# Row scaling, expert outputs and the first two units put in another order in a one-core attention, mixture-of-experts and feed-forward kernel

## The chip, the cores and the metric

The kernel runs on one core of one Trainium2 chip, in one launch. The metric is the device time of that launch in microseconds (us). Its inputs and its output lie in the chip's memory; weights are read in fp32.

## What is computed

The reference has three stages, one behind the other, over 1536 tokens (2 sequences of 768) of 512 features (8 heads of 64):

```python
# 1. linear attention with a decaying state, token by token
state = gamma * state + outer(k[t], v[t]);   y[t] = scale * (q[t] @ state)
# 2. mixture of experts: one of 8 for each token, at most `capacity` tokens each
e = argmax(x @ w_gate);  gate = softmax(x @ w_gate)[e]
out = gate * (relu(x @ w1[e]) @ w2[e])            # 512 -> 1024 -> 512
# 3. feed-forward with a rational activation
h = x @ w_in                                      # 512 -> 2048
g = (a0 + a1*h + a2*h^2 + a3*h^3) / (1 + |b0|*|h| + |b1|*h^2 + 1e-6)
out = g @ w_out                                   # 2048 -> 512
```

## The kernel before, in words

Everything runs in one hand-ordered program: the order in which the Python code calls the engines is the order of each engine's queue, and each engine takes its queue strictly in turn. The engines are TensorE (PE, with its weight loads as PEld), VectorE (DVE), ScalarE (ACT), GpSimd (POOL), and SyncE (SP), whose queue issues most transfers.

**Attention** works on 12 units of 128 tokens (`attention`, L614). A unit has a features part (k and q, transposed; chunk 0 of `kv`, 512 KB) and a tokens part (v, then k; chunk 1, 512 KB). Unit 0 takes its v from the table `c0`, so it needs only the k half of chunk 1 (`attn_part(0, 3)`, 256 KB). SP asks for these in a written order: features of unit 0, `c0`, the k half of unit 0, features of unit 1, the v half and the k half of unit 1 as two transfers, features of unit 2, then tables and the rest. For unit u, PE does: `inter(u)` (queries times the state, into `yt`; not for unit 0), `intra(u)` (v times the masked scores, into `yt`), `state(u)` (k times v, added to `st`, which ACT then copies to `s`), `scores(u + 1)` (into `sc`). DVE masks the scores (`scm`, L321 and L329) and POOL scales the v half of each unit (L278); `intra` needs both.

**Experts** (`moe`, L972). Expert 0 is done apart (`first_expert`); its last 96 rows leave it as `y0`. Experts 1 to 7 take 224 slots each. The rows of an expert are gathered by POOL, scaled with the gate by ACT (`x_gate`, L954, two parts j of 128 and 96 rows), and transposed by PE into a PSUM bank (`expert_x`, `tp`, L964), from which ACT makes the rounded high part `xh` and DVE the rest `xl` (L967, L968). All products are made of three matmuls on such high and low parts. An expert has four steps fp of the first layer (L994 to L996, ACT and DVE make `h` in L999 and L1000) and four steps q of the second (into two PSUM tiles `acc`, L373, called from L1021). Beside each step a half of the weights of later experts is split (`prep_next`: ACT L149, DVE L154), and a slice of the feed-forward weights is decoded (`dec_slot`). In expert e, `x_gate(e + 1, 0)` stands at fp 0 and `x_gate(e + 1, 1)` at fp 2; `expert_x(e + 1, ...)` at fp 1 and fp 3. `y_turn(y0, 1)` stands at fp 0 of expert 1: it transposes `y0` on PE into `ytp` (L850), in the same single PSUM bank (kind `xt`) that `expert_x` uses from expert 2 on, and ACT and DVE read it (L856, L857). Behind q 3, `y_pair` moves each `acc` to the expert's place among the features `yh` and `yl`: one ACT copy (L856) and two DVE operations (L857, L859) per `acc`. A branch for overfull experts (`overflow`, L1047, not taken here) stands behind q 3 of expert 3.

**Feed-forward** (`ffn_step(n)`, n = 0 to 47). Step n has 12 matmuls of the first layer (`ffn_a`, L1116 to L1118, into `h`, four banks in turn), the activation in pieces (`ffn_i` on ACT: L1129 to L1131; `ffn_p` on DVE and POOL: L1140 to L1142; `ffn_r` on ACT: L1147, L1148; `ffn_e` on DVE: L1153 to L1155; `ffn_g` on ACT and POOL: L1165, L1167), each some steps behind, and 12 matmuls of the second layer for step n - 5 (`ffn_b`, L1187 to L1189, into `o`). A bank of `h` is free when `ffn_e` has read it. Steps 0 to 3 are woven into q 0 to q 3 of expert 7. Expert 7 differs from the others: its `y_pair(0)`, `ffn_step(4)` and `y_pair(1)` come behind the loop, in this order. Then the experts' PSUM tiles are given up and the banks for `o` are opened in their place, and `ffn` goes on with step 5, whose `ffn_b(0)` is the first to write an `o`.

Of the kernel before, what the change touches and what calls it, by code (L numbers as in the profile page):

```python
# [7 lines left out]
F32 = mybir.dt.float32  # L8
# [5 lines left out]
AF = mybir.ActivationFunctionType  # L14
ALU = mybir.AluOpType
# [6 lines left out]
E = 8  # L22
# [62 lines left out]
class Build:  # L85
# [528 lines left out]
    def attention(self):  # L614
        nc, tc, a = self.nc, self.tc, self.a
        with ExitStack() as st:
            self.ap = self.pool("attn", stack=st)
            self.pa = self.pool("pa", space=PSUM, stack=st)
            self.kv, self.sc, self.scm, self.s, self.yt, self.xt = {}, {}, {}, {}, {}, {}
            self.route, self.place, self.xk, self.rk, self.where = {}, {}, {}, {}, {}  # L620
            self.qd, self.yp = {}, {}
            n0, n1 = self.cols["ident"][0], self.cols["tri"][0]
            nk = self.cols["gk"][0]
            self.c0 = self.ap.tile([128, -(-(nk + H * D) // 32) * 32], F32, name="c0")[:, 0 : nk + H * D]
            self.ca = self.ap.tile([128, -(-(n0 - nk) // 32) * 32], F32, name="ca")[:, 0 : n0 - nk]
            self.wi = self.ap.tile([128, 4, 256], F32, name="wi")[:, :, 0:136]
            self.tri = self.ap.tile([128, 128], BF16, name="tri")
            self.ones = self.ap.tile([128, 128], BF16, name="ones")
            self.lgs = self.ap.tile([128, NU, 4, E], F32, name="lgs")
            self.xg0 = self.ap.tile([128, DM], F32, name="xg0")  # L630
            self.x0 = [self.ap.tile([128, 4, 128], F32R, name=n) for n in ("xh0", "xl0")]
            self.wu = self.ap.tile([128, 128], BF16, name="wu")
            self.attn_load(0, 0)
            nc.sync.dma_start(out=self.c0, in_=a["c0"])
            self.attn_part(0, 3)
            self.attn_load(1, 0)
            self.attn_part(1, 2)
            self.attn_part(1, 3)
            self.attn_load(2, 0)
            nc.sync.dma_start(out=self.ca[:, 0 : n1 - nk], in_=a["ct"][:, nk:n1])  # L640
            nc.sync.dma_start(out=self.ct, in_=a["ct"][:, n0:])
            self.attn_load(2, 1)
            for c in range(2):
                self.attn_load(3, c)
            nc.sync.dma_start(out=self.ca[:, n1 - nk :], in_=a["ct"][:, n1:n0])
            dve, pool = nc.vector, nc.gpsimd
            dve.memset(self.wu, 0.0)
            dve.memset(self.ones, 1.0)
            self.warm(WA)
            self.scores(0)  # L650
            self.mask_first()
            for h in (0, 4):
                self.scale(0, pool, slice(h, h + 4))
            self.y_table(0, pool)
            self.scale(1, pool)
            self.y_table(1, pool)
            self.warm(WC)
            ident = self.col("ident").unsqueeze(1).to_broadcast([128, 4, 128])
            wg = self.col("wg").rearrange("p (k e) -> p k e", e=E)
            done = {GROUPS[b + 1] - 1: b for b in range(len(GROUPS) - 1)}  # L660
            for u in range(NU):
                last = u == NU - 1
                if u + 4 < NU:
                    for c in range(2):
                        self.attn_load(u + 4, c)
                self.load_next(LOADS[u])
                if u + 2 < UA + 3:
                    self.scale(u + 2, pool)
                if u + 2 < UPB:
                    self.y_table(u + 2, pool)  # L670
                for n in LO_AT.get(u, ()):
                    self.split_lo(n // 2, n % 2)
                if 3 < u < NU - 1:
                    self.scores(u + 1)
                    self.mask(u + 1)
                if u - 2 in done:
                    next(gate)
                self.inter(u)
                if u - 4 in done:
                    self.place_first()  # L680
                if u == 3:
                    self.scores(u + 1)
                    self.mask(u + 1)
                self.intra(u)
                if u:
                    self.attn_xt(u)
                if u - 2 in done:
                    next(gate)
                self.state(u)
                if u < 3:  # L690
                    self.scores(u + 1)
                    self.mask(u + 1, 1 if u else 2)
                if u == 0:
                    self.attn_xt(0)
                    nc.scalar.activation(out=self.wi[:, :, 0:128], in_=ident, func=AF.Copy)
                    nc.scalar.activation(out=self.wi[:, :, 128:], in_=wg, func=AF.Copy)
                if u == 3:
                    nc.scalar.activation(out=self.tri, in_=self.col("tri"), func=AF.Copy)
                    nc.scalar.activation(out=self.b0a, in_=self.ab[:, 4:5], func=AF.Abs)
                    nc.scalar.activation(out=self.b1a, in_=self.ab[:, 5:6], func=AF.Abs)  # L700
                    nc.vector.memset(self.cq, 1.0 + 1e-6)
                if u:
                    self.gate_mm(u - 1)
                if u - 2 in done and not last:
                    self.rank_mm(done[u - 2])
                if 0 < u < NU - 1:
                    self.gate_out(u - 1, (0,))
                for n in LO_MID.get(u, ()):
                    self.split_lo(n // 2, n % 2)
                if u - 1 in done:  # L710
                    gate = self.gate_parts(done[u - 1])
                    next(gate)
                if 0 < u < NU - 1:
                    self.gate_out(u - 1, (1,))
                if UA + 3 <= u + 2 < NU:
                    self.scale_heads(u + 2)
                for n in HI_AT.get(u, ()):
                    self.split_hi(n // 2, n % 2)
                if u - 2 in done and not last:
                    self.rank_pos(done[u - 2])  # L720
                if u - 3 in done and not last:
                    self.rank_put(done[u - 3])
                    self.gate_put(done[u - 3])
                for n in LO_END.get(u, ()):
                    self.split_lo(n // 2, n % 2)
            self.attn_tail()
# [123 lines left out]
            self.nc.tensor.transpose(tp[:, k], y[:, k * 128 : k * 128 + 128], self.col("ident")[0:r, 0:r])  # L850
        self.y_put(tp, slice(0, 4), bass.ds(self.start(0), r) if j else slice(0, r))

    def y_put(self, ps, k, at, more=None):
        yh, yl = self.yh[:, k, at], self.yl[:, k, at]
        tt = self.nc.vector.tensor_tensor
        self.nc.scalar.activation(out=yh, in_=ps, func=AF.Copy)  # L856
        tt(out=yl if more is None else yl.bitcast(F32), in0=ps, in1=yh.bitcast(F32), op=ALU.subtract)  # L857
        if more is not None:
            tt(out=yl, in0=more, in1=yl.bitcast(F32), op=ALU.add)  # L859

    def start(self, e):
        lo, hi = (max(0, NT - (E - e) * W), NT) if e else (0, 128)
# [109 lines left out]
    def moe(self):  # L972
        nc = self.nc
        with ExitStack() as st:
# [8 lines left out]
            for e in range(1, E):  # L983
                xh, xl = (t.pop(e)[:, :, 0:W] for t in (self.xh, self.xl))
                h = {}
                for fp in range(4):
# [14 lines left out]
                        out=hl, in0=ps, scalar=0.0, in1=hh.bitcast(F32), op0=ALU.max, op1=ALU.subtract  # L1001
                    )
                    self.prep_next()
                    if fp < 3 and fp != 1 and e + 1 < E:
                        self.x_gate(e + 1, fp // 2)
                    if fp % 2 and e + 1 < E:
                        self.expert_x(e + 1, fp // 2)
                        if e + 2 < E:
                            self.gather(2 * (e + 2) + fp // 2)
                    self.dec_slot(8 * e + fp)  # L1010
                    if (e, fp) == (1, 0):
                        self.y_turn(self.y0, 1)
                acc = [self.wide(i, "acc").rearrange("p (o n) -> p o n", o=2)[:, :, 0 : 2 * W] for i in range(2)]
                acc = [t.rearrange("p o (a n) -> p o a n", a=2) for t in acc]
                for q in range(4):
# [13 lines left out]
                        self.perm_get()  # L1029
                    if q == 3:  # L1030
                        at = bass.ds(self.start(e), W)
                        for i in range(2 if e < E - 1 else 0):
                            self.y_pair(acc, i, at)
                    self.dec_slot(8 * e + 4 + q)
                    if e == E - 1:
                        self.ffn_step(q)
                    if q % 2:
                        del self.whi[4 * e + 2 + q // 2], self.wlo[4 * e + 2 + q // 2]
            for i in range(2):
                self.y_pair(acc, i, at)  # L1040
                if i == 0:
                    self.ffn_step(4)

    def y_pair(self, acc, i, at):
        self.y_put(acc[i][:, :, 0], slice(2 * i, 2 * i + 2), at, acc[i][:, :, 1])

    def overflow(self):  # L1047
        nc, tc = self.nc, self.tc
# [179 lines left out]
    def ffn(self):  # L1228
        with ExitStack() as st:
            self.fp = self.pool("ffn", stack=st)  # L1230
            self.pf = self.pool("pf", space=PSUM, stack=st)
            for n in range(5, NA):
                self.ffn_step(n)
            self.ffn_tail()

# [178 lines left out]
```

## Time and profile before

| | before |
|---|---|
| median of 3 runs (lowest, highest) | 514.39 us (513.76, 514.82) |
| the profiled execution's own time | 512.93 us |
| its span, first to last instruction | 511.2 us |
| PE busy | 496.5 us, 97% of the span |
| DVE, ACT, POOL busy | 413.9, 365.4, 243.5 us |
| mean granted clock of PE | 0.996 of full speed |

Busy time of an engine is the time in which one of its instructions runs. Idle time counts for the end of the program only on an engine that has no idle time to spare later, so the table is read together with the rows below, which say where PE stands still and what it waits for.

### The profile page before, as it was taken

The numbers are of one execution on the slowest core, as the hardware profiler recorded it, in microseconds if no ns is written. First come the engines' busy times: TensorE is split into PE (matmuls) and PEld (weight loads), VectorE is DVE, ScalarE is ACT, GpSimd is POOL, SyncE is SP. The second block draws the span as 40 slices with busy tenths as digits, with TensorE's granted clock in tenths as the row PEclk, the third lists the DMA queues.
The fourth block names the chain that finished last, engine by engine and source line by source line (L and its number), as shares of the span: only waits on it lengthen the run. The fifth ranks groups of instructions, "written<-read, shape, count | busy, mean of one in ns | idle before, by whom it ended". The sixth has DMA issues, their size and how long they took to land.

```text
span 511.2 us, 9195 instructions
## 1 busy us (share of the span) xinstructions
PE 496.5 (97%) x3401; PEld 430.9 (84%) x3401; DVE 413.9 (81%) x602; ACT 365.4 (71%) x605; POOL 243.5 (48%) x187
## 2 busy tenths in 40 slices
PE   8999999999999999999879999999999999999995
PEld 5888878999999999998668888888888888888883
DVE  2579858789997999894686989999899998865973
ACT  1356638868767677664857989989999987776760
POOL 2621041034243744543424547667568764354774
PEclk9999999999999999999989999999999999999999
DMA  8999676899987999971400002222013100000203
GB/s 304 408 414 388 215 226 205 325 324 297 320 298 225 382 306 269 322 243 30 164 0 2 0 4 79 83 82 83 27 58 113 52 1 0 2 1 0 83 21 144
DMA packets 27409, 83.07 MB, mean 163 GB/s; under 512 B 4960, under 2 KB 5216, under 8 KB 27360
## 3 DMA queue, kind: packets, MB, share of 16 engines
q1 hardware_dynamic: 24304, 73.52, 42.2%
q0 software_dynamic: 2624, 7.35, 4.1%
q10 hardware_dynamic: 432, 1.57, 1.0%
q8 instruction: 27, 0.44, 0.3%
q14 instruction: 22, 0.18, 0.1%
HBM read 71.94 MB, written 10.49 MB: 161 GB/s over the span
## 4 chain that ended last, share of the span: by engine, by line
PE 62%; DVE 3%; ACT 2%; POOL 1%; issue 1%; POOLq 0%; ACTq 0%; DVEq 0%
PE h L1116 8%; PE h L1117 8%; PE h L1118 8%; PE o L1187 8%; PE o L1188 8%; PE o L1189 8%; PE acc L373 7%; PE e L996 2%; PE e L995 2%; PE e L994 2%; POOL out L1218 1%; PE tp L964 1%; DVE fw L1153 1%; DVE h L1154 1%; ACT fx L1129 0%
## 5 line engine op out<-in xcount | busy, mean ns | idle before, releaser
L154 DVE TENSOR_TENSOR wlo<-raw,whi 128x1024 fp32r<-128x1024 f32 x80 | 112.5, 1418 | 12.8 <-ACT whi L149 12.3
L1167 POOL TENSOR_TENSOR gg<-fx,gg 128x512 fp32r<-128x512 f32 x47 | 61.0, 1299 | 76.1 <-issue 60.8
L149 ACT ACTIVATE whi<-raw 128x1024 fp32r<-128x1024 f32 x80 | 83.2, 1056 | 2.0 <-PE acc L373 1.3
L1187 PE MATMUL o<-whi,gg 128*128 128x512 f32 x192 | 75.5, 393 | 4.6 <-DVE yl L859 4.6
L1188 PE MATMUL o<-wlo,gg 128*128 128x512 f32 x192 | 75.2, 392 | 0.0
L1189 PE MATMUL o<-whi,gg 128*128 128x512 f32 x192 | 75.2, 392 | 0.0
L1116 PE MATMUL h<-yh,whi 128*128 128x512 f32 x192 | 74.8, 390 | 0.0
L1118 PE MATMUL h<-yh,wlo 128*128 128x512 f32 x192 | 74.8, 389 | 0.0
L1117 PE MATMUL h<-yl,whi 128*128 128x512 f32 x192 | 74.7, 389 | 0.0
L373 PE MATMUL acc<-h,whi 128*128 128x448 f32 x224 | 71.3, 377 | 0.0
L1142 POOL TENSOR_TENSOR fw<-fh,fw 128x512 f32<-128x512 f32 x48 | 64.2, 1338 | 12.8 <-ACT fw L1131 12.0
L1129 ACT ACTIVATE fx<-h,ct 128x512 f32<-128x512 f32 x48 | 37.3, 777 | 42.9 <-PE h L1118 41.2
L209 POOL TENSOR_TENSOR gq<-gq 128x512 int32<-128x512 int32 x16 | 26.9, 1684 | 85.0 <-DVE gq L206 38.7
L994 PE MATMUL e<-xh,whi 128*128 128x224 f32 x224 | 62.1, 277 | 0.1
L996 PE MATMUL e<-xh,wlo 128*128 128x224 f32 x224 | 61.5, 274 | 0.0
L995 PE MATMUL e<-xl,whi 128*128 128x224 f32 x224 | 61.5, 274 | 0.0
L373 PE MATMUL acc<-h,wlo 128*128 128x224 f32 x224 | 59.0, 263 | 0.0
L1187 PEld LDWEIGHTS o<-whi,gg 128*128 128x128 f32 x192 | 36.4, 190 | 13.0 <-ACT fh L1130 5.0
L373 PEld LDWEIGHTS acc<-h,whi 128*128 128x128 f32 x224 | 42.0, 187 | 3.2
L994 PEld LDWEIGHTS e<-xh,whi 128*128 128x128 f32 x224 | 43.0, 192 | 0.5 <-ACT yh L856 0.4
L1153 DVE SCALAR_TENSOR_TENSOR fw<-fw,cq,h 128x512 f32<-128x512 f32 x48 | 35.6, 741 | 9.7 <-ACT h L1148 9.7
L995 PEld LDWEIGHTS e<-xl,whi 128*128 128x128 f32 x224 | 43.0, 192 | 0.0
(167 smaller groups left out, 1111.3 us busy)
## 6 DMA issues: line engine op xcount, KB each, us to landing
raw<-wm SPq DMA_DIRECT2D x61, 512.0 KB
r<-wf SPq DMA_DIRECT2D x32, 512.0 KB
kv<-kv SPq DMA_DIRECT2D x22, 512.0 KB
wd<-gq SPq DMA_DIRECT2D x16, 256.0 KB
raw<-wd SPq DMA_DIRECT2D x8, 512.0 KB
xd<-xs SPq DMA_DIRECT2D x12, 256.0 KB
raw<-wm ACTq DMA_DIRECT2D x3, 512.0 KB
kv<-kv SPq DMA_DIRECT2D x3, 256.0 KB
```

Of the source, the lines that this page charges most:

```text
L149: nc.scalar.activation(out=self.whi[i][:, sl], in_=raw, func=AF.Copy)
L154: (eng or self.nc.vector).tensor_tensor(out=self.wlo[i][:, sl], in0=raw, in1=self.whi[i][:, sl].bitcast(F32), op=ALU.subtract)
L373: self.nc.tensor.matmul(out, lhsT=w, rhs=x, start=start, stop=stop, skip_group_check=True)
L994: nc.tensor.matmul(ps[:, fi], lhsT=wh[:, sl], rhs=xh[:, k], start=(k == 0), stop=False)
L995: nc.tensor.matmul(ps[:, fi], lhsT=wh[:, sl], rhs=xl[:, k], start=False, stop=False)
L996: nc.tensor.matmul(ps[:, fi], lhsT=wl[:, sl], rhs=xh[:, k], start=False, stop=(k == 3))
L1116: nc.tensor.matmul(h, lhsT=wh[:, sl], rhs=self.yh[:, k, ts], start=(k == 0), stop=False)
L1117: nc.tensor.matmul(h, lhsT=wh[:, sl], rhs=self.yl[:, k, ts], start=False, stop=False)
L1118: nc.tensor.matmul(h, lhsT=wl[:, sl], rhs=self.yh[:, k, ts], start=False, stop=(k == 3))
L1187: self.nc.tensor.matmul(ps, lhsT=gh[:, ms], rhs=wh[:, ws], start=first, stop=False)
L1188: self.nc.tensor.matmul(ps, lhsT=gh[:, ms], rhs=wl[:, ws], start=False, stop=False)
L1189: self.nc.tensor.matmul(ps, lhsT=gl[:, ms], rhs=wh[:, ws], start=False, stop=last)
```

## The change

Four edits, in the order of the program:

- Start: SP asks for unit 1's features ahead of the k half of unit 0, and for unit 1's tokens as one transfer of 512 KB in the place of two of 256 KB. On PE `scores(1)` (and its mask on DVE) stands ahead of `state(0)`.
- Row scaling: `x_gate(e, 0)` for e from 3 on stands at q 2 of expert e - 2, and no longer at fp 0 of expert e - 1. `x_gate(2, 0)` stays at fp 0 of expert 1, behind `dec_slot`.
- `y_turn(y0, 1)` moves from fp 0 to q 0 of expert 1.
- Experts' end: `y_pair` is divided into `y_high` (the ACT copy) and `y_low` (the two DVE operations). For experts 1 to 6 the order on each engine is as before. For expert 7 both copies stand ahead of `ffn_step(3)`, all four DVE operations right behind it, and `ffn_step(4)` behind them, after the new banks are opened.

```diff
             nc.sync.dma_start(out=self.c0, in_=a["c0"])
+            self.attn_load(1, 0)
             self.attn_part(0, 3)
-            self.attn_load(1, 0)
-            self.attn_part(1, 2)
-            self.attn_part(1, 3)
+            self.attn_load(1, 1)
             self.attn_load(2, 0)
...
-                self.state(u)
+                if u:
+                    self.state(u)
                 if u < 3:
                     self.scores(u + 1)
                     self.mask(u + 1, 1 if u else 2)
+                if u == 0:
+                    self.state(u)
...
-    def y_put(self, ps, k, at, more=None):
+    def y_put(self, ps, k, at):
         yh, yl = self.yh[:, k, at], self.yl[:, k, at]
-        tt = self.nc.vector.tensor_tensor
         self.nc.scalar.activation(out=yh, in_=ps, func=AF.Copy)
-        tt(out=yl if more is None else yl.bitcast(F32), in0=ps, in1=yh.bitcast(F32), op=ALU.subtract)
-        if more is not None:
-            tt(out=yl, in0=more, in1=yl.bitcast(F32), op=ALU.add)
+        self.nc.vector.tensor_tensor(out=yl, in0=ps, in1=yh.bitcast(F32), op=ALU.subtract)
+
+    def y_high(self, acc, k, at):
+        self.nc.scalar.activation(out=self.yh[:, k, at], in_=acc[:, :, 0], func=AF.Copy)
+
+    def y_low(self, acc, k, at):
+        yh, yl, tt = self.yh[:, k, at], self.yl[:, k, at], self.nc.vector.tensor_tensor
+        tt(out=yl.bitcast(F32), in0=acc[:, :, 0], in1=yh.bitcast(F32), op=ALU.subtract)
+        tt(out=yl, in0=acc[:, :, 1], in1=yl.bitcast(F32), op=ALU.add)
...
-                    if fp < 3 and fp != 1 and e + 1 < E:
-                        self.x_gate(e + 1, fp // 2)
+                    if fp == 2 and e + 1 < E:
+                        self.x_gate(e + 1, 1)
...
                     if (e, fp) == (1, 0):
-                        self.y_turn(self.y0, 1)
+                        self.x_gate(2, 0)
...
                     if q == 3:
                         at = bass.ds(self.start(e), W)
-                        for i in range(2 if e < E - 1 else 0):
-                            self.y_pair(acc, i, at)
+                        y = [(acc[i], slice(2 * i, 2 * i + 2), at) for i in range(2)]
+                        for t in y:
+                            self.y_high(*t)
+                            if e < E - 1:
+                                self.y_low(*t)
+                    if (e, q) == (1, 0):
+                        self.y_turn(self.y0, 1)
+                    if q == 2 and e + 2 < E:
+                        self.x_gate(e + 2, 0)
                     self.dec_slot(8 * e + 4 + q)
                     if e == E - 1:
                         self.ffn_step(q)
...
-            for i in range(2):
-                self.y_pair(acc, i, at)
-                if i == 0:
-                    self.ffn_step(4)
+            for t in y:
+                self.y_low(*t)
...
-            for n in range(5, NA):
+            for n in range(4, NA):
                 self.ffn_step(n)
```

## Rows read from the trace of the kernel before

**Rows 1.** Busy time in stretches; after the engines the granted clock, DMA share, GB/s
```profile
12.00:43.00 31.00, 31.00 (x586) 27.36 (x583) 21.65 (x34) 14.06 (x49) 13.75 (x13) 1.00 1.03 412
84.00:100.00 16.00, 15.39 (x130) 15.06 (x129) 12.18 (x15) 13.26 (x20) 0.00 (x0) 1.00 0.94 341
...
258.20:500.00 241.80, 241.78 (x1059) 199.78 (x1060) 207.72 (x294) 197.94 (x311) 145.60 (x111) 0.99 0.11 38
```

**Rows 2.** Waits of PE over the whole span: us in total, times, longest
```profile
PE o L1187 <- DVE yl L859: 4.6, 1, 4.6
...
PE tp L964 <- ACT xg L954: 0.8, 1, 0.8
PE sc L373 <- DMA kv<-kv: 0.7, 1, 0.7
PE tp L964 <- DVE yl L857: 0.6, 1, 0.6
```

**Rows 3.** Timeline of PE at the experts' end: start, us, instruction, idle before
```profile
247.99 0.40 PE L1116 MATMUL h<-yh,whi 128*128 128x512 f32 x1
...
253.25 0.39 PE L1118 MATMUL h<-yh,wlo 128*128 128x512 f32 x1
258.20 0.77 PE L1187 MATMUL o<-whi,gg 128*128 128x512 f32 x1 [4.56 <-DVE yl L859]
...
261.22 0.40 PE L1188 MATMUL o<-wlo,gg 128*128 128x512 f32 x1
```

**Rows 4.** Busy time in the stretch of the lower granted clock
```profile
257.67:261.09 3.42, 2.89 (x7) 2.35 (x8) 3.35 (x6) 2.42 (x4) 2.14 (x2) 0.50 0.00 0
```

**Rows 5.** Timeline of ACT at the experts' end
```profile
245.68 0.60 ACT L1148 ACTIVATE h<-fh 128x512 f32<-128x512 f32 x1
247.76 0.64 ACT L1165 ACTIVATE gg<-fx 128x512 fp32r<-128x512 f32 x1 [1.49 <-DVE fx L1155]
...
251.59 0.53 ACT L856 ACTIVATE yh<-acc 128x448 f32 x1
```

**Rows 6.** Timeline of DVE at the experts' end
```profile
249.09 0.69 DVE L1155 SCALAR_TENSOR_TENSOR fx<-fw,h 128x512 f32<-128x512 f32 x1
252.15 0.62 DVE L857 TENSOR_TENSOR yl<-acc,yh 128x448 f32 x1 [2.38 <-ACT yh L856]
...
257.43 0.62 DVE L859 TENSOR_TENSOR yl<-acc,yl 128x448 f32 x1
```

**Rows 7.** Timeline of POOL at the experts' end
```profile
248.48 1.30 POOL L1167 TENSOR_TENSOR gg<-fx,gg 128x512 fp32r<-128x512 f32 x1 [2.07 <-ACT gg L1165]
```

**Rows 8.** Timeline of PE in expert 1, first matmul of its q 1
```profile
99.21 0.37 PE L373 MATMUL acc<-h,whi 128*128 128x448 f32 x1
```

**Rows 9.** Timeline of DVE in expert 1
```profile
99.58 0.55 DVE L968 TENSOR_TENSOR xl<-tp,xh 128x384 fp32r<-128x384 f32 x1
```

**Rows 10.** Waits of all engines from 84 to 108 us
```profile
ACT h L999 <- PE e L996: 2.5, 2, 2.0
```

**Rows 11.** Timeline of PE at the start
```profile
7.26 0.66 PE L373 MATMUL st<-c,kv 128*64 128x64 f32 x16
8.63 1.16 PE L373 MATMUL sc<-kv 64*128 64x128 f32 x16 [0.71 <-DMA kv<-kv]
9.72 0.67 PE L373 MATMUL yt<-kv,s 64*64 64x128 f32 x16
10.62 1.21 PE L373 MATMUL yt<-scm,kv 128*64 128x128 f32 x16 [0.23 <-issue]
```

**Rows 12.** Timeline of ACT at the start
```profile
7.96 0.38 ACT L344 ACTIVATE s<-st 128x256 f32<-128x256 f32 x1 [5.92 <-PE st L373]
```

**Rows 13.** Timeline of POOL at the start
```profile
9.23 1.04 POOL L278 TENSOR_TENSOR kv<-kv,c 128x512 f32<-128x512 f32 x1 [2.91 <-DMA kv<-kv]
```

**Rows 14.** Timeline of the SP queue at the start
```profile
9.87 0.33 SPq L247 DMA_DIRECT2D kv<-kv  x1
```

**Rows 15.** Busy time, DMA share and GB/s in one stretch of the start
```profile
5.00:6.00 1.00, 1.00 (x13) 0.66 (x11) 0.63 (x2) 0.00 (x0) 0.85 (x2) 1.00 0.70 156
```

More of the change, by code (lines that the diff above doesn't have):

```diff
@@ L1038, in moe @@
                         del self.whi[4 * e + 2 + q // 2], self.wlo[4 * e + 2 + q // 2]
-            for i in range(2):
-                self.y_pair(acc, i, at)
-                if i == 0:
-                    self.ffn_step(4)
-    def y_pair(self, acc, i, at):
-        self.y_put(acc[i][:, :, 0], slice(2 * i, 2 * i + 2), at, acc[i][:, :, 1])
+            for t in y:
+                self.y_low(*t)
     def overflow(self):
```

## The prediction

> **What bounds the kernel now.** I read the page's busy times first (PE 97%), then the busy time in stretches, then PE's waits, then the timelines around each wait. The stretches show PE busy without a gap from 12 to 43 us and, but for 0.02 us, from 258.2 to 500 us [rows 1]. So PE is the bound nearly everywhere, and the reader should take one rule from it: what makes PE stand still less, or longer, moves the end by as much, since no later stretch has room on PE to give it back. PE's waits are few [rows 2]: one of 4.6 us at the experts' end, 0.8 and 0.6 us at two row transposes (`tp`), 0.7 us for unit 1's features. The change touches all four. The wait of 4.6 us has a second price: 4.0 us after PE ended its last `h` matmul (253.25 + 0.39 = 253.64 us) the granted clock fell to half, 1.2 GHz, until 261.09 us [rows 3, 4].
>
> **The change part by part.**
>
> *Experts' end.* PE ends `ffn_a(5)` at 253.64 and then waits for the last DVE read of `acc`, which ends at 257.43 + 0.62 = 258.05 [rows 3, 6]. That read is late since ACT's copies stand behind `ffn_step(3)` and `ffn_step(4)`: DVE had nothing to do for 2.38 us until the first copy of 251.59 was done [rows 5, 6].
> After the change both copies come ahead of `ffn_g(0)`. ACT is free at 245.68 + 0.60 = 246.28 and `ffn_g(0)` starts at 247.76, after a wait of 1.49 us for DVE [rows 5]. Two copies of 0.53 us, 1.1 to 1.2 us with their gap, end near 247.5, so `ffn_g(0)` is not moved; cover left 0.3 us, and without cover `ffn_step(3)` on ACT would start up to 1.2 us later. The last `acc` matmul is issued before 247.99, the start of `ffn_a(4)`, by 12 matmuls of `ffn_a(3)`; 23 matmuls go from 247.99 to 253.25 us, 0.229 us each [rows 3], so it was issued near 245.2 and the copies needn't wait.
> DVE ends `ffn_e(1)` at 249.09 + 0.69 = 249.78 and then does the four operations, 4 x 0.62 us = 2.5 us, until 252.3 [rows 6]. `o`'s banks are thus free 1.3 us before PE asks for them at 253.6. The other input of `ffn_b(0)`, POOL's part of `ffn_g(0)`, ends at 249.78 [rows 7]. So PE goes on at once: 4.56 us gone. The clock's fall goes with it: from 258.20 to 261.22 PE issued 7 matmuls in 3.02 us; at 0.229 us these take 1.60, so 1.4 us more [rows 3]. Sum here: -6.0 us. Bounds: -6.2, and -4.0 if something else stops PE for 2 us.
> What is late next: `ffn_a(6)` needs the bank that `ffn_e(2)` frees. DVE does `ffn_p(3)` from 252.3 (two operations) and `ffn_e(2)` (three); five operations at about 0.7 us, as L1155's 0.69 [rows 6], take 3.5 us, until 255.8. PE asks at 253.6 + 12 x 0.229 = 256.4. Cover 0.6 us. In the same way `ffn_e(3)` ends near 259.3 for a need at 261.9, so the room grows from step to step. `ffn_step(4)` behind the new banks adds nothing: its matmuls write `h` banks, and `ffn_a(5)`, which stood behind the new banks already, ran at 250.8, long before 258.05.
>
> *Row scaling.* The one wait of PE for `xg`, 0.8 us [rows 2], is that of expert 4 for `x_gate(5, 0)`, which ACT reaches late, behind the untaken branch. At q 2 of expert 3 it lies ahead of the branch: -0.8 us. For the other experts PE had no such wait, and the 0.7 us of one scaling on ACT go into q 2, where ACT has idle time. New wait: ACT stands for the gather of the rows of expert e + 2, asked for at fp 1 of expert e; behind it queue the copies of `acc` and the next expert's `h`. PE's order puts two steps of the first layer and three of the second between the asking and the use, so POOL would have to be late by most of that. I take nothing; bounds 0 and +1.
>
> *`y_turn`.* At fp 0 of expert 1 it made PE wait 0.61 us: the next `tp` uses its bank, which DVE still read [rows 2]. That goes: -0.6. At q 0 it needs the bank of `tp` of the second row part. DVE's read of that starts at 99.58 and ends at 100.13 [rows 9], while PE's q 1 began at 99.21 [rows 8]: PE stands there for 100.13 - 99.21 = 0.9 us, 1.0 with the hand-over. Both sides of the gap move earlier together, since ACT itself waits for PE's first-layer steps here [rows 10]. Its transposes and its ACT and DVE operations are moved, not added; DVE's 0.55 us fall among weight splits that run several steps ahead of their use. Sum: +0.4; bounds -0.6 (DVE first) and +0.5.
>
> *Start.* The transfers are served in the order asked, at 412 GB/s when nothing disturbs them [rows 1]. The order ahead of unit 1's features loses 0.26 MB, 0.6 us: `scores(1)` starts at 8.0 in place of 8.63 [rows 11]. The k half of unit 0 then lands at about 8.6, where the features did. PE: scores until 9.1, `state(0)` 0.66 us until 9.75, ACT's copy 0.38 until 10.2 [rows 11, 12], `inter(1)` 0.67 less its overlap with the next until 10.8 [rows 11]. But `intra(1)` also needs POOL's scaled v. Its own transfer was in at 9.2 [rows 13]. Now v comes with k, and k was in when SP issued again at 9.87 [rows 14]; POOL's 1.04 us then end at 10.95, and `intra(1)` starts at 11.0, not 10.62 [rows 11]. It waits less inside (1.21 us had about 0.1 of waiting for the second mask). Sum: +0.3 us. One transfer fewer also saves SP an issue; SP is ahead of the transfers, so nothing.
> Bounds: from 5 to 6 us only 156 GB/s were moved [rows 15], 0.6 us lost; if the new order avoids that, everything is 0.6 earlier and the sum is -0.4. If the long transfer's last piece straggles, +0.6.
> The Trainium skill, "DMA: Bandwidth & Descriptors", section "Why a DMA increments its semaphore by 16 and not by 1", speaks against this edit: only the full count says that the data is in, so the first half of a joined transfer can't be used when it lands. By that rule v waits for k, as in my sum; if v could be used at 9.2 as now, `intra(1)` would follow `inter(1)` at 10.8 and the sum would be +0.1. The rows hold only the divided transfer, so they don't decide between the two.
>
> *Sum.* -6.0 - 0.8 + 0.4 + 0.3 = -6.1 us. The profiled execution took 512.93 us (span 511.2, 1.7 around it), 1.5 below the median of the runs, 514.39. So 506.8 for an execution like the profiled one, and 508.3 for the median, which is what I forecast.
>
> **The rivals.**
>
> *A part of the wait comes back.* The cover of 0.6 us ahead of `ffn_a(6)` is thin, and so is ACT's 0.3 us. If the four DVE operations start 2 us late, `o`'s banks come at 254.3, 0.7 after PE asks, and `ffn_e(2)` at 257.8, which by then is 0.7 after need: PE stands 1.4 us, and 509.7 comes out. For it: three engines hand over within 8 us. Against: both covers come from ends of operations in the rows.
>
> *The wait moves and doesn't go.* If `ffn_a(4)`, now behind the exchange of banks, had to wait for `acc` too, PE would stand from 248.2 to 252.3, 4.1 us; charged with the same 1.4 us of slow clock, 24 matmuls at 0.229 put `ffn_b(0)` at 259.2. It was at 258.2 with 1.4 still to lose, so -0.4 there, -0.5 in all: 513.9, no change. Against: `ffn_a(5)` already ran behind the exchange without that wait.
>
> *PE is tied to the weight loads (slower).* The bank that `y_turn` needs at q 0 is read by DVE behind a weight split, and ACT's half of that split needs a load. DMA is at 0.94 of its time from 84 to 100 us [rows 1]. Now a late load costs nothing there, since PE passes; behind the change PE stands with it, 1 us for each us of lateness. The gains without it are 0.6 + 6.0 + 0.8 - 0.3 = 7.1 us, so from 7.1 us of standing there (6 us of lateness) the kernel is slower; at 9 us it is 516.3. Against: among the waits of this stretch ACT's is for PE, 2.5 us [rows 10], and none is for a load.
>
> *The start and `y_turn` go well.* If the slow stretch at 5 us goes and DVE is first at q 0, -0.4 and -0.6 stand in the place of +0.3 and +0.4: 506.6. For the first: the slow second follows the first short transfer. Against the second: the order of DVE's queue.
>
> **How the numbers follow.** Forecast 0.73 (508.3; by itself 507.2 to 509.4, from the small bounds), part of the wait back 0.12 (509.7), start and `y_turn` well 0.07 (506.6), wait moved 0.05 (513.9), tied to loads 0.03 (516.3). The range 506.5 to 510.8 takes in the first three with the bounds of their terms and leaves out the last two and a stop of more than 2 us. A measurement can tell 0.2%, 1.0 us, from no change: faster 0.92 (the first three cases), the same 0.05, slower 0.03.
>
> **What would show it.** Right: no PE wait for `yl` at L1187 and `ffn_b(0)` within 0.2 us of the end of `ffn_a(5)`; no stretch at a granted clock of 0.50 there; both `yh` copies of expert 7 between `ffn_r(1)` and `ffn_g(0)`; no wait of `tp` for `xg`; a wait of about 1.0 us of PE at L850 for DVE's `xl`; `intra(1)` at 11.0 us, behind POOL. Wrong: a PE wait at L1116 for `yl` or for L1155, a wait of ACT at L954 for a gather, or `intra(1)` before 10.6 us.

## The result and the profile after

The changed kernel takes 507.16 us (median of 4 runs, 506.25 to 508.60) against 514.61 us of the kernel before beside it (4 runs, 513.76 to 517.39): ratio 0.985, interval 0.981 to 0.989. The profiled execution took 507.05 us (span 505.3, mean granted clock 0.996), 5.9 us less than that of before.

PE's waits over the whole span of the kernel after, in us in total, times, longest; they answer to [rows 2]:

```profile
PE ytp L852 <- DVE xl L975: 1.1, 1, 1.1
PE wp L302 <- DVE wu L646: 1.0, 1, 1.0
PE tp L971 <- DVE xl L975: 0.9, 1, 0.9
PE yt L373 <- ACT s L344: 0.5, 1, 0.5
PE tp L533 <- DVE rr L527: 0.3, 1, 0.3
PE yt L373 <- POOL kv L278: 0.3, 1, 0.3
```

All four waits of [rows 2] are gone: that of `o` for `yl` at the experts' end, of `tp` for `xg`, of `tp` for `yl`, of `sc` for unit 1's features. In their place stand 1.1 us at `ytp` and 0.5 and 0.3 us at the start, which were foretold, and 0.9 us of a `tp` for `xl`, which was not. The waits at `wp` and for `rr` stood there before too, with the same 1.0 and 0.3 us.

The experts' end on PE, after (timeline: start, us, instruction; it answers to [rows 3]):

```profile
253.56 0.39 PE L1127 MATMUL h<-yh,wlo 128*128 128x512 f32 x1
253.79 0.39 PE L1196 MATMUL o<-whi,gg 128*128 128x512 f32 x1
...
255.37 0.39 PE L1197 MATMUL o<-wlo,gg 128*128 128x512 f32 x1
...
256.51 0.39 PE L1125 MATMUL h<-yh,whi 128*128 128x512 f32 x1
```

The last `h` matmul of `ffn_a(5)` comes 0.31 us later than before (253.25), the first `o` matmul 0.23 us behind it, which is 4.41 us earlier than before, and the eighth `o` matmul 5.85 us earlier (261.22 before). The other engines there, ACT and then DVE, against [rows 5, 6]:

```profile
246.52 0.96 ACT L861 ACTIVATE yh<-acc 128x448 f32 x2
248.07 0.64 ACT L1174 ACTIVATE gg<-fx 128x512 fp32r<-128x512 f32 x1 [0.59 <-DVE fx L1164]
```

```profile
249.40 0.69 DVE L1164 SCALAR_TENSOR_TENSOR fx<-fw,h 128x512 f32<-128x512 f32 x1
250.00 0.62 DVE L865 TENSOR_TENSOR yl<-acc,yh 128x448 f32 x1
...
251.85 0.62 DVE L866 TENSOR_TENSOR yl<-acc,yl 128x448 f32 x1
...
255.21 0.69 DVE L1164 SCALAR_TENSOR_TENSOR fx<-fw,h 128x512 f32<-128x512 f32 x1
```

Both copies, 0.96 us together, fit into ACT's idle time (1.49 us before, 0.59 left), DVE gives up `acc` at 252.47, 1.3 us before PE asks, and `ffn_e(2)` ends at 255.90, 0.6 us before `ffn_a(6)` needs its bank at 256.51.

Busy time in stretches after (columns as in [rows 1, 4]):

```profile
248.00:260.00 12.00, 12.00 (x55) 9.88 (x54) 11.72 (x20) 11.73 (x19) 6.80 (x6) 1.00 0.10 40
252.00:494.00 242.00, 241.98 (x1068) 200.16 (x1067) 211.43 (x300) 203.51 (x319) 147.87 (x114) 1.00 0.11 37
```

PE has no gap and a granted clock of 1.00 at the experts' end, where it was 0.50 for 3.42 us [rows 4]; from 252 us on it is as full as from 258.2 us before.

### The profile page after: what moved, and what is told of

Read it like the earlier page. It is cut to its first block, busy times and chain, and to the rows that moved or that the text cites. A ratio compares the mean times of both kernels' runs of the same rounds, so it can differ in the third digit from the quotient of the medians.

```text
span 505.3 us, 9192 instructions
## 1 busy us (share of the span) xinstructions
PE 494.8 (98%) x3401; PEld 430.2 (85%) x3401; DVE 413.3 (82%) x602; ACT 365.9 (72%) x605; POOL 242.7 (48%) x187
## 4 chain that ended last, share of the span: by engine, by line
PE 64%; DVE 2%; issue 1%; ACT 1%; POOL 1%; POOLq 0%; DVEq 0%
PE h L1127 9%; PE h L1125 9%; PE h L1126 9%; PE acc L373 8%; PE o L1198 8%; PE o L1196 8%; PE o L1197 8%; PE e L1001 3%; PE e L1002 2%; PE e L1003 2%; POOL out L1227 1%; PE tp L971 0%; DVE wlo L154 0%; DVE fw L1162 0%; DVE fx L1164 0%
## 5 line engine op out<-in xcount | busy, mean ns | idle before, releaser
L1196 PE MATMUL o<-whi,gg 128*128 128x512 f32 x192 | 74.8, 390 | 0.0
L1197 PE MATMUL o<-wlo,gg 128*128 128x512 f32 x192 | 74.7, 389 | 0.0
L1003 PEld LDWEIGHTS e<-xh,wlo 128*128 128x128 f32 x224 | 43.0, 192 | 0.0
L373 PEld LDWEIGHTS acc<-h,wlo 128*128 128x128 f32 x224 | 42.7, 191 | 0.1
```

Source lines behind the costliest of these rows:

```text
L373: self.nc.tensor.matmul(out, lhsT=w, rhs=x, start=start, stop=stop, skip_group_check=True)
L1003: nc.tensor.matmul(ps[:, fi], lhsT=wl[:, sl], rhs=xh[:, k], start=False, stop=(k == 3))
L1196: self.nc.tensor.matmul(ps, lhsT=gh[:, ms], rhs=wh[:, ws], start=first, stop=False)
L1197: self.nc.tensor.matmul(ps, lhsT=gh[:, ms], rhs=wl[:, ws], start=False, stop=False)
```

## The experiments

Each is a full kernel, timed in five rounds beside the kernel before (medians 514.1 to 514.3 us there). Where nothing else is said, its time is set against the 506.92 us of the first experiment. In code and rows `...` stands for lines left out.

**The changed kernel again**, as the measure for the others.

> The changed kernel once more, to see what of its profile stays from run to run. Theory: the sum of the prediction holds, 1.1 to 1.5% under the kernel before; the wait of PE of 1.1 us at y_turn's transposes and none at L1196 come again. The wait of 0.9 us in expert 6 (tp, for DVE's xl), which the prediction did not have, hangs on when a store of a decoded slice lands (ACT stood 3.5 us for it in expert 5), so it need not come again; the rival is that the change of order brings it, then it comes again in the same place with 0.5 to 1.2 us.

Measured: 506.92 us (506.71 to 507.35), ratio 0.985 [0.982, 0.988]. In its profile PE stands 0.8 us at `ytp` and not at L1196. In expert 6 it stands 0.6 us for an `h` of ACT and not for `xl`, and 0.4 us for `xl` in expert 4: these waits move from execution to execution.

**The experts' end alone**: the kernel before with the fourth edit only. Against the changed kernel the other three are undone:

```diff
-            self.attn_load(1, 0)
             self.attn_part(0, 3)
-            self.attn_load(1, 1)
+            self.attn_load(1, 0)
+            self.attn_part(1, 2)
+            self.attn_part(1, 3)
...
-                    if fp == 2 and e + 1 < E:
-                        self.x_gate(e + 1, 1)
+                    if fp < 3 and fp != 1 and e + 1 < E:
+                        self.x_gate(e + 1, fp // 2)
...
                     if (e, fp) == (1, 0):
-                        self.x_gate(2, 0)
+                        self.y_turn(self.y0, 1)
...
```

> The kernel before with the experts' end alone changed (both copies of acc ahead of ffn_step(3), the four DVE operations behind it, ffn_step(4) behind them). Theory: this is the whole of the gain, 4.6 us of waiting and 1.4 us of slow clock, so 6.0 us (1.17%) under the kernel before; the rest of the change is worth less than 1 us together, so within 1 us of the changed kernel. Rival: the other edits carry a part of the 7.2 us (start, row scaling), then this kernel is more than 1.5 us over the changed one.

Measured: 507.40 us (506.21 to 507.76), 6.8 below before and 0.5 above the changed kernel. Its waits of PE:

```profile
PE tp L969 <- ACT xg L959: 1.2, 1, 1.2
...
PE sc L373 <- DMA kv<-kv: 0.7, 1, 0.7
PE tp L969 <- DVE yl L856: 0.6, 1, 0.6
```

The three small waits of before are there and the large one is not. The end is nearly the whole gain. The other three edits together give 0.5 us between the medians, with ranges that overlap (506.21 to 507.76 here, 506.71 to 507.35 there), so a gain by them is not shown.

**`acc` given up in two parts**: `y_low` of the second `acc` behind `ffn_step(4)`.

```diff
-            for t in y:
-                self.y_low(*t)
+            self.y_low(*y[0])
+            self.ffn_step(4)
+            self.y_low(*y[1])
...
-            for n in range(4, NA):
+            for n in range(5, NA):
```

> The changed kernel with the second acc's two DVE operations behind ffn_step(4) again, the copies early. Theory: DVE then does ffn_p(3) and ffn_e(2) first (five operations, 3.5 us, free from 251.3), so it reads the second acc until about 256.0 and PE starts L1196 at 256.1, 2.4 us late; no fall of the clock in a standstill of this length (none showed in those up to 1.1 us), so 2.4 us (0.5%) over the changed kernel. Rival: the banks of the first acc are free in time and only the first is needed, so nothing is lost.

Measured: 508.48 us (507.96 to 511.79), 1.6 more than the changed kernel and less than the 2.4 expected. PE's longest wait in it, the last DVE reads of the first and of the second `acc`, and the busy time behind the wait:

```profile
PE o L1197 <- DVE yl L866: 2.1, 1, 2.1
```

```profile
249.40 0.62 DVE L866 TENSOR_TENSOR yl<-acc,yl 128x448 f32 x1
...
254.02 0.62 DVE L866 TENSOR_TENSOR yl<-acc,yl 128x448 f32 x1
```

```profile
255.00:258.00 3.00, 3.00 (x14) 2.44 (x14) 2.93 (x6) 2.94 (x6) 0.87 (x1) 1.00 0.00 0
```

The wait is back where the order of DVE's queue puts it. It stands at the first matmul of `o` (L1197 of this kernel is L1196 of the changed one), which starts at 254.79, behind the last read of the second `acc` (254.64), though the first `acc` was read by 250.02: the early reads of the first did not help. In this profile the standstill of 2.1 us was not followed by a lower clock. But two of the six runs took 510.97 and 511.79 us at a mean clock of 0.994, the other four 507.96 to 508.77 at 0.996 or 0.997, so the clock may have fallen behind it in those two; no profile shows them.

**The copies late**: both behind `ffn_step(3)`, still ahead of step 4.

```diff
-                        for t in y:
+                        for t in y if e < E - 1 else ():
...
+            for t in y:
+                self.y_high(*t)
```

> The changed kernel with both copies (ACT) behind ffn_step(3), and all of it still ahead of ffn_step(4). Theory: the copies start at 251.9, when ffn_r(2) is done, and DVE ends the four operations at about 254.9, 1.1 us after PE asks at 253.8; ffn_e(2) also ends 2.5 us later, at 258.4, while PE asks for its bank at 257.6, so 1.1 to 2.0 us (0.2 to 0.4%) over the changed kernel. Rival: ACT's order does not count, since DVE's four operations alone fill the time: then within 0.3 us of it.

Measured: 508.72 us (507.98 to 510.58), 1.8 more. Its waits of PE:

```profile
PE o L1196 <- DVE yl L866: 1.1, 1, 1.1
...
PE h L1125 <- DVE fx L1164: 0.3, 1, 0.3
```

Both halves of the prediction's first rival stand here: the bank of `o` is late, and `ffn_a(6)` then waits for `ffn_e(2)`.

**The wait filled**: the kernel before, in which PE multiplies zeros into a bank during the wait. These 18 matmuls add nothing to any output. Against the kernel before:

```diff
-        c.tile([128, 8], F32, name="align")
...
+        self.z0 = c.tile([128, 128], BF16, name="z0")
+        nc.vector.memset(self.z0, 0.0)
...
+        if n == 5:
+            for _ in range(18):
+                z = self.z0.unsqueeze(1).to_broadcast([128, 4, 128])
+                self.nc.tensor.matmul(self.el[n], lhsT=self.z0, rhs=z, start=False, stop=False, skip_group_check=True)
```

> The kernel before with 18 matmuls of zeros (128x512, added to the last h bank) behind ffn_a(5), where PE stands 4.6 us: they add nothing to the result. Theory: PE's wait for yl stays, but PE is not idle ahead of it, so the granted clock does not fall and ffn_b(0) runs at full speed: 1.4 us (0.27%) under the kernel before. Rival: the low clock is not due to the standstill, then the slow stretch stays and the time is that of the kernel before, or over it, as ffn_i(5) waits for the zeros.

Measured: 512.12 us (510.92 to 513.34), 2.0 less than before, ratio 0.995 [0.994, 0.997]. Two stretches, PE's fill and what followed, and the wait that was left:

```profile
253.00:258.00 5.00, 5.00 (x25) 2.90 (x24) 4.01 (x7) 4.93 (x9) 3.08 (x3) 1.00 0.00 0
258.00:261.00 3.00, 2.29 (x11) 1.30 (x10) 2.93 (x5) 1.79 (x4) 0.00 (x0) 1.00 0.00 0
```

```profile
PE o L1188 <- DVE yl L860: 0.7, 1, 0.7
```

PE waits for `yl` as before, only busy. The clock stays at 1.00 and 2.0 us come back: that is the price of the lower clock by itself, in the median of its executions. It comes from the standstill.

**The start as before**, the other edits kept.

```diff
-            self.attn_load(1, 0)
             self.attn_part(0, 3)
-            self.attn_load(1, 1)
+            self.attn_load(1, 0)
+            self.attn_part(1, 2)
+            self.attn_part(1, 3)
...
-                if u:
-                    self.state(u)
+                self.state(u)
...
-                if u == 0:
-                    self.state(u)
```

> The changed kernel with the start as before (order of the transfers, state(0) ahead of scores(1)). Theory: the new start costs 0.2 to 0.3 us at intra(1) (10.92 in place of 10.62 us) and PE has no room to give it back, so 0.2 to 0.3 us less than the changed kernel. Rival: PE's matmuls stood 0.2 us late at 12 us but 0.25 us early from 52 us on, so something between 43 and 52 us, and not the start, sets the time there, and the start is worth nothing or the new one is better by 0.2 us.

Measured: 507.30 us (506.53 to 508.11), 0.4 more than the changed kernel, with the ranges overlapping. In its profile `intra(1)` starts at 11.12 us, in those of the changed kernel at 10.92 and 10.65, in that of before at 10.62 [rows 11]. The expected loss of the new start is not there; a small gain can't be told from nothing.

**`x_gate` as before** (`x_gate(e + 1, 0)` at fp 0), the other edits kept.

```diff
-                    if fp == 2 and e + 1 < E:
-                        self.x_gate(e + 1, 1)
+                    if fp < 3 and fp != 1 and e + 1 < E:
+                        self.x_gate(e + 1, fp // 2)
...
-                    if (e, fp) == (1, 0):
-                        self.x_gate(2, 0)
...
-                    if q == 2 and e + 2 < E:
-                        self.x_gate(e + 2, 0)
```

> The changed kernel with every x_gate(e, 0) back at fp 0 of expert e - 1; y_turn stays at q 0. Theory: PE's wait for xg in expert 4, behind the untaken branch, comes back with 0.8 us, and nothing else changes: 0.8 us (0.15%) over the changed kernel. Rival: at q 2 the scaling stands in the way of ACT's decode and split work and that brought the wait of 0.9 us in expert 6; then that wait goes as the other comes, and the time stays within 0.3 us of the changed kernel.

Measured: 507.47 us (506.76 to 508.43), 0.55 more between the medians, with the ranges overlapping. Its waits at `tp`:

```profile
PE tp L971 <- DVE xl L975: 0.8, 1, 0.8
...
PE tp L971 <- ACT xg L961: 0.3, 1, 0.3
```

The wait for `xg` returns with 0.3 us, not 0.8, and the one for `xl` in expert 6 stays, so the moved scaling did not bring that one.

**`y_turn` one step later**, at q 1 of expert 1.

```diff
-                    if (e, q) == (1, 0):
+                    if (e, q) == (1, 1):
                         self.y_turn(self.y0, 1)
```

> The changed kernel with y_turn one step later, at q 1 of expert 1. Theory: at q 0 PE stands 1.1 us for the bank that DVE's xl still reads (DVE ends it 1 us after PE's q 0 ends); 2.5 us later the bank is free, so that wait is gone and the time is 1.0 to 1.1 us (0.2%) under the changed kernel. Rival: the wait is one for DVE's queue in general, which is full there; then PE waits as long at q 1, and the time stays as it is.

Measured: 505.35 us (504.88 to 507.40), ratio 0.982 [0.979, 0.985]: 1.6 less than the changed kernel, and the fastest of all versions. Its profile, taken on the slowest of its runs, has no wait at `ytp`, and one in expert 6 that is longer than after:

```profile
PE tp L971 <- DVE xl L975: 1.5, 1, 1.5
```

The other five runs lie between 504.88 and 505.69.

**What holds expert 6.** ACT and then DVE ahead of its late `tp`, after:

```profile
194.09 0.67 ACT L197 ACTIVATE gq<-r 128x512 f32<-128x512 f32 x1 [3.53 <-DMA wd<-gq]
```

```profile
196.29 1.23 DVE L154 TENSOR_TENSOR wlo<-raw,whi 128x1024 fp32r<-128x1024 f32 x1 [3.11 <-ACT whi L149]
...
205.16 0.68 DVE L975 TENSOR_TENSOR xl<-tp,xh 128x512 fp32r<-128x512 f32 x1
205.76 0.61 DVE L1007 SCALAR_TENSOR_TENSOR h<-e,h 128x448 fp32r<-128x448 f32 x1
```

Busy time of the last 16 us of this, after (columns as in [rows 1]):

```profile
200.00:216.00 16.00, 15.13 (x111) 14.54 (x111) 15.90 (x19) 11.70 (x16) 6.47 (x5) 1.00 0.88 276
```

ACT stands 3.53 us for the store of a decoded slice (`wd`), whose buffer it writes next; before, this stop was 1.42 us. DVE stands 3.11 us behind ACT, then works without a break (15.90 of 16 us), and reaches `xl` at 205.16. PE stands 0.87 us ahead of `tp`, which goes at 205.98. The wait goes with the stop in every profile whose stores stand as in the kernel before: in the six with a stop of 3.26 us or more PE stands 0.6 to 1.5 us in expert 6, in the four with one of 2.85 us or less it does not. The order of the row scaling does not decide it. The fill, in which all else is ordered as before, has a stop of 4.43 us and a wait of 0.80 us; `acc` given up in two parts, with all the new orders, has 1.16 us and none. From issue to landing the stores of the kernel after took, in us:

```profile
DMA to landing us min/median/max: 3.0/6.6/10.3
```

Four experiments tried to mend this, two with the store issued by POOL in the place of SP:

```diff
-        self.nc.sync.dma_start(out=self.wd[i][:, s * 512 : s * 512 + 512], in_=self.w32.pop(n))
+        self.nc.gpsimd.dma_start(out=self.wd[i][:, s * 512 : s * 512 + 512], in_=self.w32.pop(n))
```

> The changed kernel with the stores of the decoded slices on GpSimd's queue alone (y_turn at q 0). Theory: as above, PE's waits at tp in experts 4 and 6 (1.0 us together in the second profile of the changed kernel) go, PE's 0.8 to 1.1 us at y_turn stay: 0.3 to 1.0 us under the changed kernel (506.92). Rival: transfers are late on any queue, the time stays within 0.3 us or rises.

Measured: 514.37 us (513.10 to 518.23), ratio 1.001 [0.999, 1.003]: the whole gain is lost. And with `y_turn` at q 1:

> The changed kernel with y_turn at q 1 of expert 1 and the stores of the decoded slices (dec_store, 14 to 16 stores of 256 KB) asked for on GpSimd's queue in the place of SyncE's. Theory: in the profiles of the changed kernel ACT stood 3.3 to 3.5 us in expert 5 for such a store, which lay behind four loads in SP's queue and landed 10.3 us after its issue; DVE was late by that and PE stood 0.4 to 1.5 us at a tp in experts 4 and 6. On a queue of its own the store lands earlier, ACT's wait falls under 1 us, PE's waits at tp go, and the time is 0.3 to 1.0 us under that of y_turn at q 1 alone (505.35). Rival: the 16 transfer engines themselves are full there (0.8 of their time), so the store is as late on any queue, or the loads are late in its place, and the time stays within 0.3 us or rises.

Measured: 513.95 us (512.30 to 516.63), ratio 1.000 [0.998, 1.002]. The first of the two, with `y_turn` at q 0: PE's longest wait, then ACT, then busy time in stretches:

```profile
PE tp L971 <- ACT xg L961: 3.7, 1, 3.7
```

```profile
183.94 0.67 ACT L197 ACTIVATE gq<-r 128x512 f32<-128x512 f32 x1 [5.55 <-issue]
...
188.27 0.73 ACT L961 ACTIVATE xg<-xg,tab 128x512 f32<-128x512 f32 x1
```

```profile
185.40:189.06 3.66, 0.00 (x1) 0.01 (x1) 3.09 (x5) 3.66 (x7) 0.00 (x0) 0.88 0.41 158
189.06:194.60 5.54, 5.54 (x20) 5.19 (x21) 5.54 (x7) 4.75 (x7) 4.55 (x4) 0.50 0.71 236
```

ACT stands 5.55 us at the `gq` of the eleventh slice (the 3.53 us of the changed kernel are at the thirteenth). The profile names no releaser there; the store of that buffer was issued at 174.03 and landed at 183.86. In the changed kernel SP issued the store of the same slice at 169.00, and it landed at 174.60. So on POOL's queue it was issued 5.0 us later, behind POOL's own work (an add and two indirect transfers, `pd`, stand right ahead of it), and then took 9.8 us in place of 5.6. `xg` is queued behind `gq`, PE stands 3.7 us for it, and the granted clock is then 0.50 for 5.5 us, by estimate another 2.8 us at half speed: 6.5 of the 9.1 us by which this profiled execution is longer than that of the changed kernel (spans 514.4 and 505.3). In the second of the two PE stands 5.6 us at the same place. Another queue did not make the store land sooner. The Trainium skill, "DMA: Bandwidth & Descriptors", section "SWDGE vs HWDGE vs iDMA", says that transfers issued by GpSimd run on the same 16 engines as the others; the 9.8 us of this store are in keeping with it.

Then the store one slot earlier, on SP again, first in the changed kernel and then with `y_turn` at q 1:

```diff
-        if r == 0 and 1 <= k <= 16:
-            self.dec_store(k - 1)
...
+        if r == 2 and 0 <= k < 16:
+            self.dec_store(k)
         if r == 2 and 0 <= k < 14:
             self.dec_load(k + 2)
```

> Changed kernel, but each store of a decoded slice is issued one slot earlier: in the third slot of its own round, ahead of the load of the slice after next, and no longer in the first slot of the next round. All results are computed as before. Theory (expert 6's 0.9 us wait comes from the landing of the store: in the changed kernel it was issued at 183.71 and ScalarE's gq, which writes the same buffer, stood 3.53 us until 194.09; one slot is some 2 to 3 us): ScalarE's idle time ahead of gq falls under 1 us, the wait of the transposes for xl in expert 6 goes, and the time falls by 0.5 to 0.9 us from the changed kernel's 506.9 to 507.2, to 506.3. Rival (the DMA engines are the limit in this stretch, share 0.8 to 1.0: on GpSimd's own queue a store took 9.8 us as well, 174.03 to 183.86; what is asked for earlier lands no earlier, and SyncE now stands for the add on GpSimd with loads behind it): 506.9 to 508.5, with a wait of ScalarE or VectorE for a weight load in place of the wait for the store.

> The same earlier store, with the turn of expert 1's rows in the second quarter (1, 1) as in the experiment that gave 505.35 us. Theory: five of that kernel's six runs were at 504.9 to 505.7 and one at 507.4 with a wait of 1.5 us in expert 6; with the store a slot earlier that wait goes, so its runs lie at 504.2 to 505.2, median 504.8. Rival (the wait moves to the loads): 505.3 to 507.0, and expert 6's wait stays in the profile or stands one load later.

Measured: 510.47 us (508.60 to 511.28) and 509.29 us (508.39 to 510.23), 3.6 and 3.9 more than without. SP's waits, over the span, in the first:

```profile
SPq L233 <- POOL gq L209: 77.3, 16, 6.9
```

after:

```profile
SPq L233 <- POOL gq L209: 19.7, 13, 6.2
```

and PE's longest wait in the first:

```profile
PE tp L971 <- DVE xl L975: 1.8, 1, 1.8
```

SP now stands for POOL's add with the loads queued behind it. So the stores are issued no earlier (the eleventh at 185.54, in the changed kernel at 183.71), though they take less from issue to landing (median 4.2 us against 6.6). ACT stands for no store any more, but 1.35 us for a load (`r`) at the thirteenth slice. The wait in expert 6 is gone, and one of 1.8 us stands in expert 4 (its `tp` starts at 163.51), 2.65 us in the second kernel. That follows the rival, and costs more than the rival gave; the profile of the first kernel is of the fastest of its six runs (508.60 us), so it does not hold the whole price. That the later loads are what holds expert 4 was not tested by itself. Busy time ahead of and behind the wait of the second kernel:

```profile
160.50:163.09 2.59, 0.00 (x0) 0.03 (x1) 2.59 (x3) 2.59 (x6) 2.44 (x2) 0.86 0.80 301
163.09:168.40 5.31, 5.31 (x19) 5.01 (x20) 5.28 (x8) 4.25 (x6) 2.44 (x3) 0.50 0.97 259
```

So 2.65 us of standing cost, by estimate, another 2.65 us at half speed.

## Why the prediction was right, and where it was off

**The end: right in each step.** The sum gave -6.0; the rows give 0.31 us late before it and 5.85 us early behind it, -6.2. Copies within ACT's idle time, `acc` free 1.3 us ahead of PE, cover of 0.6 us ahead of `ffn_a(6)`: all as worked out [rows 3, 5, 6]. The experiments take the three conditions away one by one: banks given up late cost 1.6 us, copies late 1.8 us, and with PE kept busy in the wait the clock does not fall. The edit alone gives 6.8 us against the kernel before, all four edits 7.2.

**Row scaling: the step right, its sum not.** The wait for `xg` is gone in the profile: at the first `tp` of expert 4 PE is 0.70 us ahead of before (155.93 against 156.63), 0.22 us behind it just ahead of that (139.72 against 139.50). But expert 6 takes it back. Its two `tp`, before and then after:

```profile
199.93 0.60 PE L964 MATMUL tp<-ct,xg 128*128 128x128 f32 x4
205.72 0.60 PE L964 MATMUL tp<-ct,xg 128*128 128x128 f32 x4
```

```profile
199.16 0.60 PE L971 MATMUL tp<-ct,xg 128*128 128x128 f32 x4
205.98 0.63 PE L971 MATMUL tp<-ct,xg 128*128 128x128 f32 x4 [0.87 <-DVE xl L975]
```

From 0.77 us ahead PE falls to 0.26 us behind, 1.03 us lost. The prediction held that no later stretch gives a gain back, from stretches that lie before 43 and behind 258 us [rows 1]; between them there was one that does, in those executions in which a store lands late. Undoing the edit costs 0.55 us between the medians, with overlapping ranges, so the 0.8 us are not shown in the time.

**`y_turn`: right.** In the profile 0.6 us went [rows 2] and 1.1 came, net +0.5 against the +0.4 foretold; in the second profile of the changed kernel 0.8 came, net +0.2. PE, then DVE:

```profile
99.02 0.55 PE L852 MATMUL ytp<-ct,y 96*128 96x96 f32 x4 [1.10 <-DVE xl L975]
```

```profile
97.28 1.22 DVE L154 TENSOR_TENSOR wlo<-raw,whi 128x1024 fp32r<-128x1024 f32 x1 [0.33 <-ACT whi L149]
98.42 0.55 DVE L975 TENSOR_TENSOR xl<-tp,xh 128x384 fp32r<-128x384 f32 x1
```

These are PE and DVE after: `xl` ends at 98.97 behind a weight split, as [rows 8, 9] had it. With the turn one step later nothing holds the bank, and that kernel is 1.6 us faster. At most 1.1 of that is this wait; where the other 0.5 comes from stays open.

**Start: the step right, its worth unproved.** `intra(1)` at 10.92 us behind POOL was foretold as 11.0, by the same chain, PE and then POOL after:

```profile
9.95 0.67 PE L373 MATMUL yt<-kv,s 64*64 64x128 f32 x16 [0.48 <-ACT s L344]
10.92 1.09 PE L373 MATMUL yt<-scm,kv 128*64 128x128 f32 x16 [0.30 <-POOL kv L278]
```

```profile
9.82 1.04 POOL L278 TENSOR_TENSOR kv<-kv,c 128x512 f32<-128x512 f32 x1 [3.69 <-DMA kv<-kv]
```

POOL starts 0.59 us later than in [rows 13], where v had a transfer of its own. The Trainium skill, "DMA: Bandwidth & Descriptors", section "Why a DMA increments its semaphore by 16 and not by 1", says that only the full count means that all of a transfer's data has landed; by that, v can't be used ahead of k. The start at 9.82 us agrees. But it is no proof: with the start undone, and v in a transfer of its own, POOL started at 9.93. Executions differ here by more than the step: in the four profiles with the old start `intra(1)` stands between 10.09 and 11.30 us, in the ten with the new one between 10.54 and 11.41. Two of the ten (10.54 and 10.56, the stores one slot earlier) lie under the 10.6 us that the prediction named as a sign of being wrong. Nor does the step reach the later work: at the first row transposes (`xtp`) PE of the kernel after is 0.25 us ahead of before (54.76 against 55.01), and not 0.3 behind. The +0.3 is not shown in the time, as a loss or as a gain.

**From the profile to the median: the term that was mis-sized.** The sum of -6.1 held for the profiled executions (-5.9), in part by luck: the 1.03 us lost in expert 6, which it did not have, are made up in the main by the start (0.25 us early in place of 0.3 late) and by an end and a row scaling that gave 0.2 and 0.1 us more. To it the prediction added the 1.5 us by which the profiled execution of before lay under its median, and the median came out 1.1 us lower than that. The mean granted clock that each run lists tells why. Of 62 runs of the kernel before beside the experiments only 2 stand at 0.996, the clock of its profiled execution; they took 512.7 and 512.9 us. 26 stand at 0.993 (median 513.8), 34 at 0.991 or less (27 at 0.990, median 514.6). So most executions of before lost more to the lower clock than the 1.4 us of the profiled one; all ten runs of the changed kernel stand at 0.996 to 0.999. That the fall at the experts' end is what varies is borne out by the end alone, whose five runs stand at 0.998 or 0.999, and by the fill, which takes only the lower clock away, stands at 0.996 to 0.998 and gives 2.0 us; but no second profile of before shows it.

Of the rivals, a returning part of the wait showed only where an experiment put it there; a wait ahead of `ffn_a(4)`, and one of PE for loads at `y_turn`, did not come.

## What to carry to other kernels

When the first user of a new set of buffers waits for the last reader of the old ones, move the readers into idle time that the rows show, and check what each of them pushes back: here 1.0 us of copies and 2.5 us of reads moved, and 6 us came back. Price a long standstill of PE with the slower clock behind it, and look at the clock of several runs, since one profile may show the cheapest fall. A stage in which a second engine has no idle time left can take small gains of PE back. Moving a transfer to another queue puts it behind the work of that queue, and moving it ahead in its own moves what waits behind it as well.

## What the runs showed of the hardware

- The granted clock was 0.50 behind standstills of 4.56 us (for 3.42 us, 2.89 of them behind it [rows 3, 4]), 3.73 us (5.54 us), 5.62 us (5.36 us, the second kernel with stores on POOL) and 2.65 us (5.31 us). It was 1.00 in the profiles behind one of 2.1 us and one of 1.8 us. How long the clock stayed low did not follow the length of the standstill.
- A store of 256 KB took 3.0 to 10.3 us to land from SP's queue in the changed kernel, among the weight loads, and one of them 9.8 us from POOL's.
